# Moving 24 fp32 transposes from the tensor engine to the DMA crossbar in a fused attention and mixture-of-experts kernel

## The chip, the cores and the metric

The kernel runs on one core of a Trainium2 chip. The metric is device time of that core in microseconds (us), lower is better. The margin for "faster" or "slower" is 2%.

The names in the profile: PE is the tensor engine's matmul, PEld its weight loads, DVE the vector engine, ACT the scalar engine, POOL is GpSimd, SP the engine that issues most of the transfers.

## The reference, cut to what matters

```python
# B=4 batches, H=8 heads, S=768 rows, D=64, 16 clusters per head
q_n, k_n, c_n = q/|q|, k/|k|, centroids/|centroids|
q_assign = argmax(einsum('bhsd,hcd->bhsc', q_n, c_n), -1)     # cluster of each query
k_assign = argmax(einsum('bhsd,hcd->bhsc', k_n, c_n), -1)     # cluster of each key
mask   = q_assign[:, :, :, None] == k_assign[:, :, None, :]
attn   = softmax(where(mask, q @ k.T / sqrt(D), -1e9))
x      = (attn @ v) as 3072 x 512
p      = domain_probs / domain_probs.sum(-1)
out    = sum over 4 experts e of p[:, e] * (relu(x @ w1[e]) @ w2[e])   # w1: 512 x 1024
```

Two things matter for the change. Keys and queries have to stand with D on the partitions, so they must be transposed. The cluster scores feed an argmax, so the kernel computes them in fp32: the transposed data must keep all its 32 bits. The two remaining uses of it, the rows for q·k, are cast to bf16.

## The kernel before

One stream of PE instructions interleaves attention, the experts' matmuls and the assignment of the next batch. The batches are numbered 0 to 3; batch 1 is the second. For each batch there are four objects: keys (z = 0) and queries (z = 1) of heads 0 to 3 (g = 0) and of heads 4 to 7 (g = 1). Two classes do the transposing. `Assign.turn` does it on PE, through PSUM (the banks that PE's results go to, from which DVE copies them here); `Crossed` does it with the DMA crossbar in 16-bit elements (the prediction says why), so POOL first splits each fp32 word in its low and high halves, both are crossed, and POOL interleaves them again. The kernel before uses `Crossed` for batches 2 and 3, and `turn` for batches 0 and 1. Each batch's assignment is a list of slots, and the slots are spread over the steps of the attention. The work on each object ends with its onehot, which marks the cluster of each row: one small crossing turns it, and POOL then issues 8 small transfers (the sends) that put it into the rows below the keys or queries. The code is cut down; `...` marks what is left out.

```python
def load_w(e):                       # one expert's weights, issued by POOL
    nc.gpsimd.dma_start(out=W1[e], ...)
    nc.gpsimd.dma_start(out=W2[e], ...)

class Assign:
    def turn(self, y, copy, ...):    # head y of the group: 3 transposes, 1 copy
        tp = self.bank()             # PSUM
        for i in range(3):
            nc.tensor.matmul(tp[:, 128*i:...], raw[b, t, g][:, y, 128*i:...],
                             ident, is_transpose=True)
        t32 = self.all[:, y*384:(y+1)*384]
        copy(t32, tp)                # DVE
    def cast(self, y, r, copy): ...  # bf16 rows for q.k, half r of the partitions (POOL)
    def scores(self, copy): ...      # 4 fp32 matmuls against the centroids, copy
    def back(self): ...              # 3 fp32 transposes of the scores
    def top(self): ...               # onehot of the best cluster (DVE)
    # cross_onehot: DMA transpose of it;  send_all: 8 small transfers, issued by POOL

class Crossed(Assign):
    def split(self, n): ...          # POOL: 128x768 uint16, one half-word plane of 2 heads
    def cross(self, j): ...          # SP: DMA transpose of 128x768 uint16
    def merge(self, n): ...          # POOL: 128x768 uint16 back into self.all
    def casts(self): ...             # DVE: bf16 rows, all four heads at once
    def scores_split(self, bank): ...# scores whose way back also goes by crossbar

def assigns(b):
    xs = [Crossed(b, t, g, ...) for t, g in ((1, 0), (0, 0), (1, 1), (0, 1))]
    def put(at, *fs): ...            # run fs in slot `at` of this batch's list
    for y, x in enumerate(xs):
        z = y % 2
        if b == 1:
            t = 12 * (y // 2) + 4 * z
            for j in range(HG):                      # HG = 4 heads
                put(t + j, lambda x=x, j=j: turn(x, j))
            put(t + 3, lambda: load_raw(upto=13))
            at = 12 * (y // 2) + 8
            put(at, lambda x=x: x.scores(dve))
            put(at + 1 + z, x.back, x.top, x.scale_onehot, x.cross_onehot)
            put(at + 4 + z, x.send_all)
        else: ...                    # split, cross, merge, casts, scores_split
    # weights of experts 2 and 3 in slots 1 and 19, V casts in slots 26 and 29

# the slots of batch 1 (31 of them) are spread evenly over the attention steps
XSTEPS = [0, 31, 63, 63]
gens.append(Paced(assigns(b), XSTEPS[b], S1 + 7, PER_B * b + 2))   # b == 1
```

The softmax here doesn't subtract the row's maximum and nothing guards it: scores larger than these inputs give would overflow.

Of the kernel before, what the change touches and what calls it, by code (L numbers as in the profile page):

```python
# [20 lines left out]
def kernel(  # L21
# [16 lines left out]
    B, H, S, D = q.shape  # L38
# [6 lines left out]
    QW = QT * 128  # L45
# [3 lines left out]
    HG = H // 2  # L49
# [24 lines left out]
    act, dve, pool = nc.scalar.copy, nc.vector.tensor_copy, nc.gpsimd.tensor_copy  # L74
# [35 lines left out]
    def late(t, b):  # L110
        x = KF[b % 2].rearrange("p h r c -> p (h r c)")
        n = NP * A * 128
        return x[:, t * n:(t + 1) * n].rearrange("p (x i r c) -> p x i r c", i=QT, r=2, c=128)
# [15 lines left out]
    def load_part(b, t, g, js=slice(0, HG), c=slice(0, A * D)):  # L129
        nc.sync.dma_start(  # L130
            out=raw[b, t, g][:, js, c],
            in_=(q, k, v)[t][b, g * HG:(g + 1) * HG]
            .rearrange("h (p a) d -> p h (a d)", p=128)[:, js, c])

    def take_raw():
        nonlocal loaded
        x = ORDER[loaded]
        loaded += 1
        raw[x] = raws.tile([128, HG, A * D], F32, name="raw")
        return x  # L140

    def load_raw(n=1, upto=len(ORDER)):
        for _ in range(n):
            if loaded < upto:
                load_part(*take_raw())

    def cast_v(b, g, js=range(HG)):
        for j in js:
            pool(VX[b % 2][:, g * HG + j, :, :D],
                 raw[b, 2, g][:, j, :].rearrange("p (a d) -> p a d", d=D))  # L150

    def load_w(e):
        nc.gpsimd.dma_start(out=W1[e], in_=moe_w1[e].rearrange("(i p) f -> p i f", p=128))
        nc.gpsimd.dma_start(out=W2[e], in_=moe_w2[e].rearrange("(i p) f -> p i f", p=128))
# [57 lines left out]
    class Assign:  # L212
# [23 lines left out]
        def turn(self, y, copy, shared=False):  # L236
            tp = self.bank()
            m, w = self.m, self.w
            for x in range(m):
                for i in range(self.i0, self.i1):  # L240
                    c0 = x * w + (i - self.i0) * 128
                    nc.tensor.matmul(tp[:, c0:c0 + 128],  # L242
                                     raw[self.b, self.t, self.g][:, y * m + x,
                                                                 i * 128:(i + 1) * 128],
                                     ident, is_transpose=True)
            if shared:
                t32 = moe.tile([128, DM], F32, name="t32q", tag="oacc", bufs=4)
            else:
                if self.all is None:
                    self.all = asg.tile([128, HG * QW], F32, name="t32", bufs=2)  # L250
                t32 = self.all[:, y * w:(y + 1) * w]
            copy(t32, tp[:, :m * w])
            self.t32s.append(t32)
# [63 lines left out]
        def put(self, j, r, on):  # L317

            p0 = 2 * CL * j
            self.move(self.rows(slice(D, D + CL), j, r),  # L320
                      self.ot[p0:p0 + CL, r * self.w:(r + 1) * self.w], on)
# [22 lines left out]
    class Crossed(Assign):  # L344


        def halves(self, x):
            return x.rearrange("p j c -> p (j c)").bitcast(U16)

        def split(self, n):  # L350
            src = self.halves(raw[self.b, self.t, self.g]).rearrange(
                "p (y j a d s) -> p s y a j d", j=2, a=A, d=D, s=2)
            if n == 0:
                self.h16 = self.halves(raws.tile([128, HG, QW], F32, name="h16", tag="raw"))
            dst = self.h16.rearrange("p (s y a j d) -> p s y a j d", s=2, a=A, j=2, d=D)
            z, y = divmod(n, HG // 2)
            if self.b == ROWS:
                pool(dst[:, z, y], src[:, z, y])  # L358
            else:
                c = y * 2 * QW  # L360
                pool(self.h16[:, z * HG * QW + c:z * HG * QW + c + 2 * QW],  # L361
                     self.halves(raw[self.b, self.t, self.g])[:, 2 * c:2 * c + 4 * QW][:, z::2])
# [20 lines left out]
        def casts(self):  # L383
            y = self.g * HG // 2
            if self.b < ROWS:
                for r in range(2):
                    dve(self.rows(slice(0, D), slice(0, HG), r),
                        self.all[D * r:D * r + D, :].rearrange("p (j c) -> p j c", j=HG))
                return
            dve(late(self.t, self.b)[:, y:y + HG // 2], self.rows_of())  # L390

        def scores_split(self, bank_tag):
            sc = bank(bank_tag)
            for x in range(HG):
                y, r = divmod(x, 2)
                if self.b == ROWS:
                    lhs, rhs = bdl[:, self.g * HG // 2 + y, :], self.rows_of()[:, y, :, r, :]
                else:
                    lhs, rhs = bdc[:, self.g * HG + x, :], self.all[:, x * QW:(x + 1) * QW]
                nc.tensor.matmul(sc[32 * x:32 * x + 32, :QW], lhs, rhs, start=True, stop=True)  # L400
            self.sch = asg.tile([128, QW], F32, name="scs").bitcast(U16)
            src = sc[:, :QW].bitcast(U16)
            for s in range(2):
                dve(self.sch[:, s * QW:(s + 1) * QW], src[:, s::2])
# [53 lines left out]
    def assigns(b):  # L458


        xs = [Crossed(b, t, g, (("misc",), ("mo",))[t == 0])
              for t, g in ((1, 0), (0, 0), (1, 1), (0, 1))]
        todo = {}

        def put(at, *fs):
            todo.setdefault(at, []).extend(fs)

        def turn(x, j):
            x.turn(j, dve)
            for r in range(2):  # L470
                x.cast(j, r, pool)

        for y, x in enumerate(xs):
            z = y % 2
            if b == 1:
                t = 12 * (y // 2) + 4 * z
                for j in range(HG):
                    put(t + j, lambda x=x, j=j: turn(x, j))
                put(t + 3, lambda: load_raw(upto=13))
                at = 12 * (y // 2) + 8  # L480
            else:
                t = 8 * y
                for j in range(HG):
                    put(t + j, lambda x=x, j=j: x.split(j))
                    put(t + 2 + j, lambda x=x, j=j: x.cross(j))
                    put(t + 9 + j, lambda x=x, j=j: x.merge(j))
                put(t + 6, load_raw)
                put(t + 15 + 4 * z, x.casts)
                at = 16 * (y // 2) + 24
            if b == 1:  # L490
                put(at, lambda x=x: x.scores(dve))
                put(at + 1 + z, x.back, x.top, x.scale_onehot, x.cross_onehot)
                put(at + 4 + z, x.send_all)
                continue
            put(at, lambda x=x, t=("mo", "misc")[z]: x.scores_split(t))
            put(at + 2 + 6 * z, x.cross_scores)
            put(at + 5 + 6 * z, x.merge_scores)
            if b < ROWS:
                put(at + 9 + 6 * z, x.top, x.scale_onehot, x.cross_onehot)
                put(at + 13 + 6 * z, x.send_all)  # L500
                continue
            put(at + 9 + 6 * z, x.top, x.number, x.cross_numbers)
            put(at + 12 + 6 * z, x.store_numbers)
            put(at + 14 + 6 * z, x.spread_numbers)
        for g in range(2):
            if b == 1:
                put(1 + 18 * g, lambda g=g: load_w(2 + g))
                put(26 + 3 * g, lambda g=g: cast_v(b, g), lambda: load_raw(upto=13))
            else:
                for j in range(HG):  # L510
                    put(36 + 8 * g + j, lambda g=g, j=j: cast_v(b, g, (j,)))
                put(40 + 8 * g, load_raw)
        for at in range(XSTEPS[b]):
            for f in todo.pop(at, []):
                f()
            yield
        assert not todo
# [248 lines left out]
    NSTEP = B * UB * PER_U + PAUSE  # L766
    PER_B = UB * PER_U
    LEAD = 6
    XSTEPS = [0, 31, 63, 63]
    step = 0  # L770
    gens = []

# [77 lines left out]
    def late_casts():  # L850
        for j in range(HG):
            cast_v(0, 1, (j,))
            if j < 2:
                casts(k1, (2 + j,))
# [35 lines left out]
    S1 = PER_U + PAUSE  # L890
    gens.append(Paced(late_queries(), 5, S1 - 6, S1 + 4))
    for b in range(1, B):
        gens.append(Paced(assigns(b), XSTEPS[b], PER_B * (b - 1) if b > 1 else S1 + 7,
                          PER_B * b - (2 if b > 1 else -2)))

    def woven(works, upto):

# [51 lines left out]
```

## Time and profile before

The time was 475.53 us (median of 3 runs, 475.3 to 476.02). The page of the profiled execution gives, in short:

| | before |
|---|---|
| span of the profiled execution | 474.3 us |
| busy share: PE / ACT / DVE / POOL | 98% / 58% / 48% / 39% |
| chain that ended last, share of PE | 94% |
| fp32 transposes of raw inputs on PE | 96, of them 48 for batch 1 (3 per head and operand) |
| POOL, from 53.85 to 63.28 us | idle, waiting for the crossed onehot |

How to read it: "busy" is the sum of an engine's instruction records over the span, and an engine can be busy without being the limit. The chain that ended last starts at the last instruction and goes back, at each step, to whatever let that instruction start. When nearly all of that chain is one engine following itself, the time of that engine's stream is the time of the kernel. The lines that show this are in the prediction.

### The profile page before, as it was taken

Reading aid. Unit: us, or ns where it says so; the run is one execution under the profiler, and the core shown is the slowest. Engines: PE = TensorE matmul, PEld = TensorE weight load, DVE = VectorE, ACT = ScalarE, POOL = GpSimd, SP = SyncE. Lnnn points to the kernel's source line nnn. Section 1 sums busy time; section 2 is a strip of 40 time slices with the busy share of each in tenths; the row PEclk is TensorE's granted clock in tenths of the full one; section 3 lists DMA queues with packets and bytes.
Section 4 is the critical chain, followed back from the end, with each engine's and each line's share of the span. In section 5 each row is a group of like instructions: output and inputs, shape, how many; then the busy total and the mean of one; then the engine's idle time right before and its main releaser. Section 6 shows DMA issues by size and latency. Waiting matters only on the chain.

```text
span 474.3 us, 11380 instructions
## 1 busy us (share of the span) xinstructions
PE 466.8 (98%) x4529; PEld 331.6 (70%) x4529; DVE 226.0 (48%) x558; ACT 277.1 (58%) x502; POOL 186.1 (39%) x301
## 2 busy tenths in 40 slices
PE   8999999999999999999999999999999999999997
PEld 4778777776776767677676767776766766667665
DVE  5964764321316664321234544423878767675112
ACT  5757655445665656566565655665665675664442
POOL 5936469180653694450442933000332132220000
PEclk9999999999999999999999999999999999999999
DMA  8999962927664940603657545202100100100101
GB/s 278 259 211 344 241 128 42 177 44 174 96 122 114 199 118 18 159 15 62 150 141 123 115 114 160 68 16 73 50 13 8 54 10 8 36 28 12 44 2 44
DMA packets 75981, 48.27 MB, mean 102 GB/s; under 512 B 51544, under 2 KB 70680, under 8 KB 75928
## 3 DMA queue, kind: packets, MB, share of 16 engines
q1 hardware_dynamic: 66680, 38.22, 32.7%
q0 software_dynamic: 8576, 9.25, 11.0%
q8 instruction: 35, 0.57, 0.6%
q10 hardware_dynamic: 672, 0.08, 0.1%
q14 instruction: 18, 0.15, 0.1%
HBM read 37.31 MB, written 6.30 MB: 92 GB/s over the span
## 4 chain that ended last, share of the span: by engine, by line
PE 94%; DVE 2%; DMA 2%; SPq 0%; issue 0%; ACT 0%; ACTq 0%
PE ps_mo L724 35%; PE ps_mo L743 35%; PE ps_s L634 9%; PE ps_av L661 7%; PE ps_s L547 1%; DMA raw<-in_q_dram 1%; DMA kf<-oht 1%; PE ps_misc L242 1%; PE ps_misc L547 1%; PE ps_misc L400 1%; PE ps_mo L400 1%; PE ps_mo L242 1%; DVE kf L315 1%; PE ps_mo L267 0%; PE ps_misc L267 0%; DVE oh L287 0%
## 5 line engine op out<-in xcount | busy, mean ns | idle before, releaser
L640 ACT ACTIVATE at<-ps_s 128x512 bf16<-128x512 f32 x252 | 147.7, 596 | 119.0 <-PE ps_s L634 103.9
L724 PE MATMUL ps_mo<-xT,w1b 128*128 128x256 bf16 (+1 forms) x1664 | 195.8, 264 | 0.0
L743 PE MATMUL ps_mo<-w2b,hT 128*128 128x512 bf16 (+2 forms) x784 | 190.3, 375 | 0.0
L724 PEld LDWEIGHTS <-w1b 128*128 128x128 bf16 x1664 | 146.3, 98 | 25.1 <-issue 1.2
L730 ACT ACTIVATE hT<-ps_mo 128x512 bf16<-128x512 f32 x192 | 114.7, 598 | 60.7 <-PE ps_mo L724 58.0
L752 DVE SCALAR_TENSOR_TENSOR oacc<-ps_mo,psb,oacc 128x512 f32<-128x512 f32 (+1 forms) x74 | 54.3, 734 | 130.7 <-PE ps_mo L743 130.4
L743 PEld LDWEIGHTS <-hT 128*128 128x128 bf16 x784 | 67.1, 98 | 57.5 <-issue 3.1
L634 PE MATMUL ps_s<-qf,kf 80*128 80x256 bf16 (+1 forms) x456 | 82.5, 267 | 0.9 <-ACT at L640 0.4
L661 PEld LDWEIGHTS <-at 128*128 128x128 bf16 x1152 | 69.9, 97 | 15.3 <-issue 1.7
L661 PE MATMUL ps_av<-vx,at 128*128 128x65 bf16 x1152 | 80.3, 193 | 0.0
L647 POOL TENSOR_TENSOR at<-at,same 128x512 bf16<-128x512 bf16 x24 | 28.2, 1174 | 98.5 <-ACT at L640 82.8
L634 PEld LDWEIGHTS <-kf 80*128 80x128 bf16 x456 | 42.0, 98 | 20.8 <-issue 1.9
L564 DVE TENSOR_SCALAR same<-qf,late 128x256 bf16<-128x256 bf16 x144 | 39.3, 324 | 0.0
L377 POOL COPY t<-t 128x768 uint16<-128x768 uint16 x32 | 35.5, 1116 | 0.0
L647 DVE TENSOR_TENSOR at<-at,same 128x512 bf16<-128x512 bf16 x48 | 21.6, 449 | 25.7 <-ACT at L640 25.7
L358 POOL COPY h<-raw 128x768 uint16<-128x768 uint16 x16 | 13.0, 825 | 37.3 <-DMA raw<-in_q_dram 30.7
L668 DVE RECIPROCAL zr<-ps_av 128x4 f32<-128x4 f32 (+1 forms) x50 | 8.9, 178 | 33.9 <-PE ps_av L661 33.8
L361 POOL COPY h<-raw 128x768 uint16<-128x768 uint16 x16 | 13.0, 826 | 28.9 <-DMA raw<-in_q_dram 20.4
L336 POOL DMA_DIRECT2D kf<-oht x32 | 15.4, 496 | 22.8 <-DMA oht<-oh 13.1
L750 DVE TENSOR_SCALAR oacc<-ps_mo,psb 128x512 f32<-128x512 f32 x18 | 13.5, 749 | 22.7 <-PE ps_mo L743 22.7
L416 POOL COPY st<-sct 128x384 uint16<-128x384 uint16 x16 | 10.6, 708 | 31.7 <-DMA sct<-scs 31.7
L336 POOL DMA_DIRECT2D qf<-oht x40 | 20.0, 509 | 6.2 <-DVE oht L313 3.9
(130 smaller groups left out, 281.5 us busy)
## 6 DMA issues: line engine op xcount, KB each, us to landing
raw<-in_v_dram SPq DMA_DIRECT2D x8, 768.0 KB, 5.7
out_dram<-oacc SPq DMA_DIRECT2D x23, 256.0 KB, 2.2
raw<-in_k_dram SPq DMA_DIRECT2D x7, 768.0 KB, 6.3
raw<-in_q_dram SPq DMA_DIRECT2D x6, 768.0 KB, 5.3
w1b<-in_moe_w_dram POOLq DMA_DIRECT2D x4, 1024.0 KB, 11.5
w2b<-in_moe_w_dram POOLq DMA_DIRECT2D x4, 1024.0 KB, 16.8
qf<-nos SPq DMA_DIRECT2D x2, 768.0 KB, 4.0
xT<-xn SPq DMA_TRANSPOSE x80, 2.4
```

Of the source, the lines that this page charges most:

```text
L336: (nc.gpsimd if self.b or self.i0 and self.g else nc.sync).dma_start(out=self.rows(slice(D, D + CL), j, r), in_=self.oht[p0:p0 + CL, :self.w])
L377: pool(self.all[:, y * w:(y + 1) * w].bitcast(U16)[:, z::2], self.t16[:, (2 * z + y) * w:(2 * z + y + 1) * w])
L564: nc.vector.tensor_scalar(same[:, x * 256:(x + 1) * 256], clusters(b)[:, g, w, k // 2, k % 2, :], key_nos[b % 2][:, g, 8 * i + 4 * (k // 2 ...
L634: nc.tensor.matmul(sp[:, x * n:(x + 1) * n], KF[b % 2][:K, h, r, i * 128:(i + 1) * 128], QF[b % 2][:K, h, rs[0]:rs[-1] + 1, w * 128:(w + 1 ...
L640: nc.scalar.activation(at, sp, ACT.Exp, scale=scale)
L647: (nc.gpsimd if n4 in POOL_STEPS else nc.vector).tensor_tensor(at, at, same_cluster(b, w, cur), op=ALU.mult)
L661: nc.tensor.matmul(av[:, h % 2, m, :], at[:, c0:c0 + 128], VX[b % 2][:, h, 2 * i + r, :], start=(first and x == 0 and m == 0), stop=(last ...
L724: nc.tensor.matmul(ph[:, x * n:(x + 1) * n], W1[e][:, i, (f + x) * 128:(f + x + 1) * 128], xT[:, i, :], start=(i == 0), stop=(i == ND - 1))
L730: nc.scalar.activation(ht, ph, ACT.Relu)
L743: nc.tensor.matmul(po, hT[f // per][:, c0:c0 + 128], W2[e][:, f, c], start=(f == 0), stop=(f == NF - 1))
L750: nc.vector.tensor_scalar_mul(oacc, po, pap)
L752: nc.vector.scalar_tensor_tensor(oacc[:, c], po, pap, oacc[:, c], op0=ALU.mult, op1=ALU.add)
```

## The change

The intent: take the 24 transposes of heads 4 to 7 of batch 1 out of PE's stream and let the crossbar, which has room, do them. Heads 0 to 3 stay on PE. The price is paid on POOL (splits and merges), on SP (eight more crossings) and in the buffers for raw inputs, which now also hold the halves; so the loads of V for heads 4 to 7 and of batch 2's first keys are issued later, and the cluster scores move from slot 20 to slot 29 of a list that has 38 slots now.

```diff
--- before.py
+++ after.py
@@ -347,6 +347,9 @@
         def halves(self, x):
             return x.rearrange("p j c -> p (j c)").bitcast(U16)
 
+        def take_all(self):
+            self.t32s = [self.all[:, j * QW:(j + 1) * QW] for j in range(HG)]
+
         def split(self, n):
             src = self.halves(raw[self.b, self.t, self.g]).rearrange(
                 "p (y j a d s) -> p s y a j d", j=2, a=A, d=D, s=2)
@@ -384,10 +387,13 @@
             y = self.g * HG // 2
             if self.b < ROWS:
                 for r in range(2):
-                    dve(self.rows(slice(0, D), slice(0, HG), r),
-                        self.all[D * r:D * r + D, :].rearrange("p (j c) -> p j c", j=HG))
+                    self.cast_half(r)
                 return
             dve(late(self.t, self.b)[:, y:y + HG // 2], self.rows_of())
+
+        def cast_half(self, r):
+            dve(self.rows(slice(0, D), slice(0, HG), r),
+                self.all[D * r:D * r + D, :].rearrange("p (j c) -> p j c", j=HG))
 
         def scores_split(self, bank_tag):
             sc = bank(bank_tag)
@@ -470,28 +476,41 @@
             for r in range(2):
                 x.cast(j, r, pool)
 
-        for y, x in enumerate(xs):
-            z = y % 2
-            if b == 1:
-                t = 12 * (y // 2) + 4 * z
-                for j in range(HG):
-                    put(t + j, lambda x=x, j=j: turn(x, j))
-                put(t + 3, lambda: load_raw(upto=13))
-                at = 12 * (y // 2) + 8
-            else:
-                t = 8 * y
-                for j in range(HG):
-                    put(t + j, lambda x=x, j=j: x.split(j))
-                    put(t + 2 + j, lambda x=x, j=j: x.cross(j))
-                    put(t + 9 + j, lambda x=x, j=j: x.merge(j))
-                put(t + 6, load_raw)
-                put(t + 15 + 4 * z, x.casts)
-                at = 16 * (y // 2) + 24
-            if b == 1:
+        if b == 1:
+            for y, x in enumerate(xs):
+                g, z = divmod(y, 2)
+                if g == 0:
+                    for j in range(HG):
+                        put(4 * z + j, lambda x=x, j=j: turn(x, j))
+                else:
+                    for j in range(HG):
+                        put((8, 14)[z] + j, lambda x=x, j=j: x.split(j))
+                        put((13, 18)[z] + j, lambda x=x, j=j: x.cross(j))
+                        put((20, 24)[z] + j, lambda x=x, j=j: x.merge(j))
+                    put((24, 28)[z], x.take_all)
+                    for r in range(2):
+                        put(28 + 3 * z + r, lambda x=x, r=r: x.cast_half(r))
+                at = (8, 29)[g]
                 put(at, lambda x=x: x.scores(dve))
                 put(at + 1 + z, x.back, x.top, x.scale_onehot, x.cross_onehot)
-                put(at + 4 + z, x.send_all)
-                continue
+                put(at + (4, 5)[g] + z, x.send_all)
+            put(1, lambda: load_w(2))
+            put(3, lambda: load_raw(upto=11))
+            put(20, lambda: cast_v(b, 0))
+            put(22, lambda: load_raw(2, upto=13))
+            put(24, lambda: load_w(3))
+            put(30, lambda: cast_v(b, 1))
+
+        for y, x in enumerate(xs if b > 1 else ()):
+            z = y % 2
+            t = 8 * y
+            for j in range(HG):
+                put(t + j, lambda x=x, j=j: x.split(j))
+                put(t + 2 + j, lambda x=x, j=j: x.cross(j))
+                put(t + 9 + j, lambda x=x, j=j: x.merge(j))
+            put(t + 6, load_raw)
+            put(t + 15 + 4 * z, x.casts)
+            at = 16 * (y // 2) + 24
             put(at, lambda x=x, t=("mo", "misc")[z]: x.scores_split(t))
             put(at + 2 + 6 * z, x.cross_scores)
             put(at + 5 + 6 * z, x.merge_scores)
@@ -502,14 +521,10 @@
             put(at + 9 + 6 * z, x.top, x.number, x.cross_numbers)
             put(at + 12 + 6 * z, x.store_numbers)
             put(at + 14 + 6 * z, x.spread_numbers)
-        for g in range(2):
-            if b == 1:
-                put(1 + 18 * g, lambda g=g: load_w(2 + g))
-                put(26 + 3 * g, lambda g=g: cast_v(b, g), lambda: load_raw(upto=13))
-            else:
-                for j in range(HG):
-                    put(36 + 8 * g + j, lambda g=g, j=j: cast_v(b, g, (j,)))
-                put(40 + 8 * g, load_raw)
+        for g in range(2 if b > 1 else 0):
+            for j in range(HG):
+                put(36 + 8 * g + j, lambda g=g, j=j: cast_v(b, g, (j,)))
+            put(40 + 8 * g, load_raw)
         for at in range(XSTEPS[b]):
             for f in todo.pop(at, []):
                 f()
@@ -766,7 +781,7 @@
     NSTEP = B * UB * PER_U + PAUSE
     PER_B = UB * PER_U
     LEAD = 6
-    XSTEPS = [0, 31, 63, 63]
+    XSTEPS = [0, 38, 63, 63]
     step = 0
     gens = []
 
@@ -891,7 +906,7 @@
     gens.append(Paced(late_queries(), 5, S1 - 6, S1 + 4))
     for b in range(1, B):
         gens.append(Paced(assigns(b), XSTEPS[b], PER_B * (b - 1) if b > 1 else S1 + 7,
-                          PER_B * b - (2 if b > 1 else -2)))
+                          PER_B * b - 2 if b > 1 else S1 + 55))
 
     def woven(works, upto):
 
```

## The prediction

> **What bounds the kernel now.** I read the page's engine table and its slices first, then the chain that ended last, then the groups of instructions with shapes kept apart, then the timeline of the stretch that the change touches. The engine table and the head of the slices:
>
> ```profile
> PE 466.8 (98%) x4529; PEld 331.6 (70%) x4529; DVE 226.0 (48%) x558; ACT 277.1 (58%) x502; POOL 186.1 (39%) x301
> ...
> PE   8999999999999999999999999999999999999997
> ...
> POOL 5936469180653694450442933000332132220000
> PEclk9999999999999999999999999999999999999999
> DMA  8999962927664940603657545202100100100101
> ```
>
> PE is busy in every slice after the first at full granted clock; no other engine is over 58%. Busy alone does not prove a bound, so the chain that ended last is what carries it:
>
> ```profile
> PE 94%; DVE 2%; DMA 2%; SPq 0%; issue 0%; ACT 0%; ACTq 0%
> ```
>
> 94% of the span is PE following PE in program order, so an instruction taken out of PE's stream in the middle of the kernel shortens the span by the time it holds that stream, as long as what replaces it is there when PE asks. In the waits of PE between 30 and 130 us there is one entry only, 0.2 us for a onehot tile. So PE has almost no waiting to give up: the gain is pure removed work, and any new wait is a pure loss.
>
> **What the Trainium skill says.** "TensorE: Matmul & The Clock Gate", Part 4, says that PE's transpose goes to PSUM, so that a copy must follow, and gives about 275 ns for a 128x128 one inside a kernel. The trace agrees on the record (273 ns for fp32) but the records overlap: three hold the stream for only 0.36 us. "DMA: Bandwidth & Descriptors", DMA Transpose (X-bar), Constraints: only 2-byte elements and only from SP or ACT. That is why the fp32 data is split in halves; in this trace the same trick in batches 2 and 3 is uint16 and issued by SP. "Trainium Kernel Development and Optimization", Key Constraints: transfers issued from SP, ACT and POOL share the same 16 DMA engines. The trace agrees: while expert 2's weights and raw loads were in flight together (45 to 57 us), the second weight half took 15.9 us to land against 13.7 us for expert 3's, alone.
>
> **The change, part by part.** It concerns keys and queries of heads 4 to 7 of batch 1. Each of the two has 4 heads x 3 blocks of 128x128, so 24 fp32 transposes leave PE. Their place is in the PE timeline, in sets of three:
>
> ```profile
> 58.46 0.52 PE L242 MATMUL ps_misc<-ident,raw 128*128 128x128 f32 x3
> 58.82 0.59 PE L743 MATMUL ps_mo<-w2b,hT 128*128 128x512 bf16 x2
> ...
> 66.71 0.53 PE L242 MATMUL ps_mo<-ident,raw 128*128 128x128 f32 x3
> 67.08 1.47 PE L724 MATMUL ps_mo<-xT,w1b 128*128 128x256 bf16 x12
> ```
>
> The cost is start to next start, not the record's 0.52: the eight sets give 0.36, 0.39, 0.33, 0.38, 0.36, 0.37, 0.38 and 0.37, in sum **2.94 us**. This lies wholly on PE's path. The fp32 cluster scores and the two transposes back stay on PE and move later: scores from position 68.82 to behind the start of expert 2's second unit.
>
> DVE loses 8 copies of 128x384 from PSUM at 0.555 us (4.4 us) and gains 4 casts of 64x1536 at 1.1 us (4.4 us): even. POOL loses 16 casts of 64x384 at 0.505 us (8.1 us) and gains 8 splits at 0.826 (6.6 us) and 8 merges at 1.04 to 1.12 (8.6 us): **7 us more**. SP's queue gains 8 crossbar transposes at 1.25 us of issue and 2.8 us to landing. Loads of V (heads 4 to 7) and of batch 2's first keys move later, because their buffers now hold the halves. Expert 3's weights are issued further on in the program. None of these is on PE's path as long as it is in time.
>
> **Is it in time?** The rows that decide it are the groups of the pieces and POOL's timeline:
>
> ```profile
> L377 POOL COPY t<-t 128x768 uint16<-128x768 uint16 x32 | 35.5, 1116 | 0.0
> L361 POOL COPY h<-raw 128x768 uint16<-128x768 uint16 x16 | 13.0, 826 | 28.9 <-DMA raw<-in_q_dram 20.4 <-DMA raw<-in_k_dram 8.4
> ...
> 63.28 3.86 POOL L336 DMA_DIRECT2D kf<-oht  x8 [9.43 <-DMA oht<-oh]
> 67.19 1.05 POOL L258 CAST kf<-t 64x384 bf16<-64x384 f32 x2
> 68.18 3.81 POOL L336 DMA_DIRECT2D qf<-oht  x8
> 72.04 3.23 POOL L258 CAST kf<-t 64x384 bf16<-64x384 f32 x6
> 75.31 4.32 POOL L258 CAST qf<-t 64x384 bf16<-64x384 f32 x8
> 79.57 0.81 POOL L153 DMA_DIRECT2D w1b<-in_moe_w_dram  x1
> ```
>
> POOL works in order and sits from 53.85 to 63.28 us waiting for the crossed onehot of heads 0 to 3. The order of the changed kernel puts the key splits into that hole (53.9 to 57.2, free), then the 16 sends, the query splits, one merge, 4 V casts, three merges, one merge of queries, expert 3's two weight issues, three merges.
>
> My clock for that. In the kernel before, the onehot transposes (issued 56.9) queue behind the V load issued at 46.63 (11.3 us) and share the engines with expert 2's weights; the change moves that V load away, so I estimate that the onehot lands at 60.5 rather than 63.3. Sends 16 x 0.49 = 7.8: to 68.3. Query splits 3.3: to 71.6. Merge 1.05 and V casts 2.0: 74.7. Three merges: 78. First query merge 79, weights 1.7: 80.8, three merges: **84.0**. The transposes of the query halves can only start at 71.6; with two xT transposes between them (2.4 us) the last is issued near 78 and lands near 81, just ahead of its merge.
>
> PE comes to those scores at: 89.93 in the timeline before (88.28, the pieces of that step, then 8 of the 24 matmuls), less 2.94, less the group's own scores (1.43) and transposes back (0.66) that no longer stand ahead of them: **84.9**. So the data is there 0.9 us ahead by my estimate, and late by 1.9 us if the onehot does not land sooner than before. That is the tightest point. Weighing these, I take a mean wait of 0.4 us.
>
> The second point is expert 3. Its issue at 79 to 80 is where it was (79.57), but V and K loads of 1.5 MB now run beside it. Alone it took 13.7 us for the second half; expert 2's, with such loads beside it, 15.9. So about 96 to 97 against PE's need at 103.47 - 2.94 = 100.5: no wait.
>
> Sum: 475.5 - 2.9 + 0.4 = **473.0 us**, 0.5% faster.
>
> **The rivals.**
> First: **PE waits at the moved scores** because POOL's 7 us more come in a stretch where POOL is already solid (63 to 84). For it: a margin below 1 us, and an in-order queue with a DMA wait at its head. Against it: the hole before 63 takes the key splits, and 16 casts go. It gives back 1 to 3 us: 474 to 476.
> Second: **expert 3's weights late**, through DMA contention or a late POOL. For it: the weights are issued behind a merge that itself waits for a transpose. Against: 3.5 us of margin. It would cost 1 to 3 us more.
> Third: **nothing takes its place**: the whole 2.94 is kept, 472.6. The slots look chosen to just fit, which speaks for it. A fourth, that removal leaves PE waiting for ACT between closer steps, I hold small: ACT is at 58% and it waits for PE 104 us at the exps.
>
> **Range and chances.** The best case is 472.6, and 0.3 us of noise in the runs makes 472.0 the low end. The bad case of the first rival, 475, is the high end; beyond it both rivals have to hit. Over 2% means under 466, four times the removed work: chance 0.01. Over 2% slower means 485, some 12 us of new stalls, which needs a wait that repeats or a load that comes far too late: 0.02.
>
> **What the profile after would show.** Right: the fp32 transposes of the stretch 58 to 67 gone (96 to 72 by count at that line); PE's time before heads 4 to 7 shorter by 2.9; PE's waits still under a microsecond; POOL's sends of the onehot starting near 60.5; merges done by 84. Wrong: a wait of PE at the scores matmul for POOL's merge (first rival), or at the first matmuls of expert 3 for its weights (second), or a span that shrinks by less than 2.9 with no wait of PE, which would say that the sets did not cost 0.36 each. The prediction fails as a whole if PE stalls by more than 2.5 us in sum, or if the time falls below 472.0, for which something besides the transposes would have to leave PE's path.

## The result, and the profile after

| | before | after |
|---|---|---|
| time, median (range) | 475.77 us (475.3 to 476.12), 4 runs | 472.21 us (472.15 to 472.63), 4 runs |
| ratio after / before, 95% interval | | 0.993 (0.9916 to 0.9944) |
| span of the profiled execution | 474.3 us | 470.4 us |

Ratios here and below are the mean time of one kernel's fast runs over the mean of the other's fast runs of the same rounds, so they are not quite the ratio of the medians quoted. The kernel is 0.7% faster and counts as the same at the 2% margin.

From the page of the changed kernel: the engine table, two rows of the 40 slices, and the engines of the chain that ended last.

```profile
PE 463.2 (98%) x4505; PEld 329.1 (70%) x4505; DVE 227.4 (48%) x554; ACT 276.9 (59%) x502; POOL 194.8 (41%) x301
...
POOL 5936779275355593450433942000233232230000
...
DMA  8999966996645941503666844220100100100101
...
PE 95%; DVE 2%; DMA 1%; issue 0%; ACT 0%; SPq 0%; ACTq 0%
```

PE has 24 matmuls fewer (4529 to 4505; the raw transposes at L242 go from 96 to 72) and 3.6 us less busy time, and is still 94 to 95% of the chain. POOL has 8.7 us more; I had counted 7. In its row the fifth to seventh digits rise from 469 to 779: the former hole, around 54 to 63 us, holds the key splits now. In the row of the DMA engines the seventh digit rises from 2 to 6, where most of the added crossings and the moved loads begin, and the ninth from 2 to 9: there expert 3's weights are still under way (they landed at 97.96 and before at 94.07), and batch 2's crossings begin at 97.4 and not at 103.2.

The timeline of PE in the changed kernel (start, duration, engine, line, operation, tiles, count), first where a set of three transposes stood, then where heads 4 to 7's scores stand:

```profile
58.18 0.29 PE L676 MATMUL ps_av<-vx,at 128*128 128x65 bf16 x4
58.31 0.59 PE L758 MATMUL ps_mo<-w2b,hT 128*128 128x512 bf16 x2
58.74 0.38 PE L649 MATMUL ps_s<-qf,kf 80*128 80x256 bf16 x2
...
84.14 0.61 PE L739 MATMUL ps_mo<-xT,w1b 128*128 128x128 bf16 x8
84.68 0.85 PE L267 MATMUL ps_misc<-t,bdc 128*32 128x384 f32 x8
85.35 0.83 PE L267 MATMUL ps_mo<-t,bdc 128*32 128x384 f32 x8
```

Before, a set of matmuls of the attention weights with V (`ps_av`) started at 58.34 and the next set of an expert's second matmuls (`w2b`) at 58.82, with the transposes at 58.46 between them; now one follows the other after 0.13 us. The scores of the keys start at 84.68, those of the queries at 85.35, and neither line carries a wait in brackets.

POOL's timeline in the changed kernel, which has to feed those scores; the bracket is the idle time before a group and what ended it:

```profile
53.75 3.13 POOL L364 COPY h<-raw 128x768 uint16<-128x768 uint16 x4
...
60.96 3.87 POOL L336 DMA_DIRECT2D kf<-oht  x8 [4.08 <-DMA oht<-oh]
65.13 3.83 POOL L336 DMA_DIRECT2D qf<-oht  x8 [0.30 <-DMA kf<-oht]
68.96 3.12 POOL L364 COPY h<-raw 128x768 uint16<-128x768 uint16 x4
...
80.33 3.73 POOL L380 COPY t<-t 128x768 uint16<-128x768 uint16 x3
```

The key splits sit where POOL was idle, the onehot came at 60.96 instead of 63.28, and the last merge ended at 80.33 + 3.73 = 84.06, which is 1.3 us before the query scores that need it.

**Where the time went.** Single spans differ by chance at the start and near the end of the program, so I measured one stretch that holds the whole change and none of that. Its first mark is POOL's pair of key casts of heads 0 to 3 near 44 us, its second the first fp32 scores of batch 3. The two marks before, and then after:

```profile
44.57 1.05 POOL L258 CAST kf<-t 64x384 bf16<-64x384 f32 x2 [0.76 <-DVE t L252]
254.10 0.85 PE L400 MATMUL ps_mo<-t,late 128*32 128x384 f32 x8
...
44.41 1.05 POOL L258 CAST kf<-t 64x384 bf16<-64x384 f32 x2 [0.77 <-DVE t L252]
250.95 0.85 PE L406 MATMUL ps_mo<-t,late 128*32 128x384 f32 x8
```

In the profile before it ran from 44.57 to 254.10, which is 209.53 us; in the one after from 44.41 to 250.95, which is 206.54. So **2.99 us of the 3.9 us between the two spans lie in the stretch**; 0.16 lie ahead of it, and 0.75 behind it (220.2 us from the second mark to the end, against 219.45). The experiments treat the 2.99 and the 0.75 separately.

### The profile page after: what moved, and what is told of

It reads as the page before. It is cut to its first block, busy times and chain, and to the rows that moved or that the text cites. A ratio compares the mean times of both kernels' runs of the same rounds, so it can differ in the third digit from the quotient of the medians.

```text
span 470.4 us, 11349 instructions
## 1 busy us (share of the span) xinstructions
PE 463.2 (98%) x4505; PEld 329.1 (70%) x4505; DVE 227.4 (48%) x554; ACT 276.9 (59%) x502; POOL 194.8 (41%) x301
## 4 chain that ended last, share of the span: by engine, by line
PE 95%; DVE 2%; DMA 1%; issue 0%; ACT 0%; SPq 0%; ACTq 0%
PE ps_mo L739 36%; PE ps_mo L758 35%; PE ps_s L649 9%; PE ps_av L676 7%; PE ps_s L562 1%; DMA kf<-oht 1%; PE ps_misc L562 1%; PE ps_s L87 1%; PE ps_mo L406 1%; PE ps_mo L242 1%; PE ps_misc L406 1%; DVE kf L315 1%; PE ps_misc L242 1%; PE ps_mo L267 0%; PE ps_misc L267 0%; DVE oh L287 0%
## 5 line engine op out<-in xcount | busy, mean ns | idle before, releaser
L745 ACT ACTIVATE hT<-ps_mo 128x512 bf16<-128x512 f32 x192 | 114.7, 598 | 60.5 <-PE ps_mo L739 57.7
L380 POOL COPY t<-t 128x768 uint16<-128x768 uint16 x40 | 44.3, 1127 | 0.0
L364 POOL COPY h<-raw 128x768 uint16<-128x768 uint16 x24 | 20.3, 864 | 30.4 <-DMA raw<-in_k_dram 16.7
L361 POOL COPY h<-raw 128x768 uint16<-128x768 uint16 x16 | 13.1, 829 | 39.3 <-DMA raw<-in_q_dram 32.3
L685 DVE TENSOR_TENSOR xn<-ps_av,zr 128x256 bf16<-128x256 f32 (+1 forms) x50 | 20.7, 414 | 1.7
```

Source lines behind the costliest of these rows:

```text
L380: pool(self.all[:, y * w:(y + 1) * w].bitcast(U16)[:, z::2], self.t16[:, (2 * z + y) * w:(2 * z + y + 1) * w])
L685: nc.vector.tensor_tensor(xn[:, :nr].rearrange("p i j d -> p j i d"), av[:, :, :, :D], zr.broadcast_to([128, 2, nr, D]), op=ALU.mult)
L745: nc.scalar.activation(ht, ph, ACT.Relu)
```

## The experiments

The theory: the gain is the time that the 24 transposes held PE's stream and nothing else, and POOL and the DMA stay ahead with a small margin. Its rivals: (a) some of the gain comes from the moved loads and the new slots, not from the removed transposes; (b) PE gains more and gives part of it back in a new wait. Later a third question came up: what the 0.75 us outside the stretch is. Every run gave a correct result.

The measure in each case is the ratio to the kernel before of the same rounds, and the stretch defined above, whose noise is shown by the controls.

### Controls: ctl_before and after_again

No edit: the kernel before, and the changed kernel, run again.

> The kernel before, unchanged, as a control. Every theory expects a ratio of 1.000 within 0.002. What it is to tell: in the profile of the kernel before, PE lost 0.7 us at the last fp32 cluster scores of batch 3 (282.90 to 284.38 us, 1.48 us for 8 matmuls where the first 8 took 0.66), because the crossed scores before landed 5.5 us after their issue; in the changed kernel they landed in 3.7 us and the wait was gone. If this wait is a property of the schedule, it shows here again; if it is chance of one execution, it is absent or of another size.

> The changed kernel, unchanged, in the same rounds as its improved version. The transposes theory, with 3.0 us saved between 44 and 254 us and nothing lasting elsewhere, expects ratio 0.9935 to 0.994; the first measurement, 0.993 over few runs, should come down toward it. If there is a lasting second gain of half a microsecond: 0.9925 to 0.993.

Measured: ctl_before 475.49 us against 475.56 (ratio 0.9996, 0.9983 to 1.001), stretch 209.54. after_again 472.17 against 475.53 (0.9928, 0.9916 to 0.994; six runs against ten), stretch 206.54. The stretch repeats within 0.01 us in both kernels (two profiles of each), so it is a far finer measure than the time of a run. The difference of the two is 3.00 us. The ratio of after_again did not come down toward 0.994 as I expected; it lies in the band that I had given to a second gain of half a microsecond. Its profile shows no such gain after the stretch, though: from the second mark to the end it took 219.5 us, as in ctl_before.

### sched_only: the new slots and loads, with the transposes still on PE

```diff
-                        put((8, 14)[z] + j, lambda x=x, j=j: x.split(j))
-                        put((13, 18)[z] + j, lambda x=x, j=j: x.cross(j))
-                        put((20, 24)[z] + j, lambda x=x, j=j: x.merge(j))
-                    put((24, 28)[z], x.take_all)
-                    for r in range(2):
-                        put(28 + 3 * z + r, lambda x=x, r=r: x.cast_half(r))
+                        put((12, 16)[z] + j, lambda x=x, j=j: turn(x, j))
```

> The schedule of the change alone (38 slots, later scores, V and K loads and weights in their new places), with heads 4 to 7 still turned by PE and cast by POOL. Transposes theory: ratio to before 0.998 to 1.000 (at most the 0.7 us wait of batch 3 goes). Rival that the schedule itself brings it: 0.993 to 0.995.

Measured: 475.36 us, ratio 0.9995 (0.9982 to 1.0007), stretch 209.54. The schedule alone is worth nothing. Rival (a) falls.

### keys_only: only the keys of heads 4 to 7 go by the crossbar

```diff
-                if g == 0:
+                if g == 0 or z == 1:
                     for j in range(HG):
-                        put(4 * z + j, lambda x=x, j=j: turn(x, j))
+                        put(12 * g + 4 * z + j, lambda x=x, j=j: turn(x, j))
```

> Only the keys of heads 4 to 7 go through the crossbar; the queries are turned by PE, in the schedule of the change. Transposes theory, linear in the sets: half of 2.94, so 1.5 us (with batch 3's wait gone 2.2): ratio 0.9955 to 0.997. Rival, all or nothing by the schedule: 0.993.

Measured: 473.43 us, ratio 0.9955 (0.9943 to 0.9968), stretch 207.99, which is 1.54 us less than before. Half of the transposes bring half of the gain: the gain is proportional to what is removed, as removed work is and as a wait need not be.

### idle_turns: the change, and 24 transposes of the identity put back on PE

The three transposes per head read and write nothing that anything waits for; they only hold the stream.

```diff
+        def idle_turn(x):
+            tp = x.bank()
+            for i in range(QT):
+                nc.tensor.matmul(tp[:, i * 128:(i + 1) * 128], ident, ident, is_transpose=True)
...
+                    for j in range(HG):
+                        put((12, 16)[z] + j, lambda x=x: idle_turn(x))
```

> The changed kernel plus the 24 fp32 transposes put back at about their old places as idle work on PE (identity into a bank that nobody reads). Theory that the gain is PE time of 24 transposes: 2.9 to 3.0 us more than the changed kernel, so about 475.2 us, ratio to before 0.999. Rival that the gain comes from the other movements (V load later, POOL and DMA order, batch 3's wait gone): stays at 472 to 473, ratio 0.993 to 0.994.

Measured: 475.05 us, ratio 0.9988 (0.9975 to 1.0001), stretch 209.30: 2.76 us of the 2.99 come back. The crossbar path is all in place here, so it is PE's stream that was relieved. The 24 idle ones cost 0.115 us each and the real ones 0.125. Of the 0.23 us between the sums, about 0.1 lies in the sets themselves: from start to next start the idle ones sum to 2.83 us. The rest was not looked for.

### scores_28: the scores of heads 4 to 7 one slot earlier

```diff
-                at = (8, 29)[g]
+                at = (8, 28)[g]
```

This tests whether the margin at the scores is small, that is whether the slot is chosen to just fit.

> The changed kernel with the moved scores, and the steps after them that hang on the same slot, one slot (about 1.26 steps) earlier. In the changed kernel the last merge ends at 84.06 and PE is at the first scores at 84.68. PE would now come to them some 2 us sooner, near 82.5. Theory of a margin of about half a microsecond: PE waits 1 to 2 us for the last merge of the queries, ratio to before 0.995 to 0.997 (473.3 to 474.2 us). Rival that PE has ample slack here: ratio stays 0.993.

Measured: 474.8 us, ratio 0.9984 (0.9972 to 0.9997), stretch 209.19, which is 2.65 us worse than the change. PE's timeline:

```profile
81.28 0.85 PE L267 MATMUL ps_misc<-t,bdc 128*32 128x384 f32 x8
81.95 0.82 PE L267 MATMUL ps_mo<-t,bdc 128*32 128x384 f32 x4
...
84.59 0.84 PE L267 MATMUL ps_mo<-t,bdc 128*32 128x384 f32 x4 [1.82 <-POOL t L380]
```

The keys' eight matmuls and half of the queries' run without a wait, and the other four start 2.64 us after those, when POOL's last merges are done. In the change they follow at once, so this wait is the whole loss. This is the first rival of my prediction, made real: one slot earlier, nearly the whole gain is gone. PE came 3.4 us earlier than in the change (81.28 against 84.68), where I had reckoned with 2, because the step between the two slots is a long block, and POOL's last merge ended at 84.53, 0.47 later than in the change; so the cost was more than I expected.

### v_early: an idle 768 KB load about where the V load was, ahead of the crossed onehot

```diff
+            put(4, lambda: nc.sync.dma_start(
+                out=W1[3].rearrange("p i f -> p (i f)").bitcast(F32)[:, :HG * A * D]
+                .rearrange("p (j c) -> p j c", j=HG),
+                in_=v[1, HG:].rearrange("h (p a) d -> p h (a d)", p=128)))
```

The real V load cannot simply go back, as its buffer holds the halves. So this loads the same bytes into the room of expert 3's first weights, which are written later. It was issued earlier than the load that it stands for: it ran from 39.62 to 55.90 us, the V load before from 46.63 to 57.88. It tests the part of the prediction that said the onehot lands sooner because the V load is gone.

> The changed kernel plus an idle load of 768 KB of V in front of the crossed onehot of heads 0 to 3 (into the room of expert 3's weights, which come later), so that the traffic there is as in the kernel before. Theory of the prediction: the onehot lands near 63.3 instead of 61.0, the merges end near 86.4, PE waits about 1.7 us at the scores: ratio to before 0.996 to 0.9975. Rival that expert 2's weights alone set the landing: 61.0 again and 0.993.

Measured: 472.79 us, ratio 0.9944 (0.9932 to 0.9957), stretch 207.63, which is 1.09 us worse than the change. POOL's timeline:

```profile
63.29 3.86 POOL L336 DMA_DIRECT2D kf<-oht  x8 [6.31 <-DMA oht<-oh]
...
82.66 2.98 POOL L380 COPY t<-t 128x768 uint16<-128x768 uint16 x3
```

And PE's timeline, at the first of expert 3's second matmuls:

```profile
101.52 1.02 PE L762 MATMUL ps_mo<-w2b,hT 128*128 128x512 bf16 x3 [0.72 <-ACT hT L749]
```

The onehot came at 63.29, within 0.01 us of where it came before the change. That the moved V load brings it forward by 2.3 us is right. The way was not quite the predicted one, a queue behind V: here the idle load had landed at 55.90, before the crossings of the onehot were issued at 57.13 and 58.74. What was late was expert 2's second weight transfer: it landed at 62.30 (62.29 before, 59.73 in the change). In all twelve profiles that transfer landed at 62.3 to 62.7 us where the V or idle load ran ahead, and at 59.7 to 60.1 where it did not, and POOL's first send of the onehot followed 0.9 to 1.3 us later. The size of the loss was not as I expected. The merges ended at 85.64 instead of 84.06, only 1.6 us later, because POOL made up some time, and PE lost 0.24 us at the query scores, not 1.7. It stood idle for 0.72 us elsewhere, at the first matmul of expert 3's second weights. The profile puts that wait down to ACT, but the transfer of those weights was issued at 81.42 and took 20.0 us to land, to 101.4. So the second rival of the prediction showed here: in the change itself that transfer was issued at 79.44, took 18.5 us and landed at 97.96, with PE needing it at 100.3, and here it was issued 2.0 us later, as POOL was late, and took 1.5 us longer. Priced from start to next start, this wait cost 0.86 us (2.22 from the start of the 24 matmuls ahead of it, against 1.36 in the change), and with the 0.24 that is the whole of the 1.09.

### scores_cross and scores_cross2: the scores' way back by crossbar too

An attempt to find a better version: the three fp32 transposes back per object (`back`) also leave PE, as in batches 2 and 3.

```diff
+                if g == 1:
+                    put(29, lambda x=x, t=("misc", "mo")[z]: x.scores_split(t))
+                    put(30 + 2 * z, x.cross_scores)
+                    put(31 + 2 * z, x.merge_scores)
+                    put(33 + 2 * z, x.top, x.scale_onehot, x.cross_onehot)
+                    put(36 + 2 * z, x.send_all)
+                    continue
...
-    XSTEPS = [0, 38, 63, 63]
+    XSTEPS = [0, 39, 63, 63]
```

> The changed kernel, and the scores of heads 4 to 7 go back through the crossbar as halves too, in place of two sets of three fp32 transposes on PE (0.33 us each). If it is in time: 0.66 us less than the changed kernel, ratio to before 0.991 to 0.992. Rival: the onehot of these heads comes too late (it passes POOL behind expert 3's weights and batch 2's keys), PE waits at heads 4 to 7, and the time is equal or up to 3 us more.

Measured: 473.46 us, ratio 0.996 (0.9946 to 0.9973), stretch 207.65: 1.11 us worse than the change, though 0.66 us of work left PE. POOL's timeline:

```profile
99.82 1.14 POOL L422 COPY st<-sct 128x384 uint16<-128x384 uint16 x2 [6.18 <-DMA sct<-scs]
```

And PE's timeline at batch 2's first query scores:

```profile
140.06 0.82 PE L406 MATMUL ps_misc<-t,bdc 128*32 128x384 f32 x4
141.81 0.84 PE L406 MATMUL ps_misc<-t,bdc 128*32 128x384 f32 x4 [0.94 <-POOL t L380]
```

POOL works in order. The first crossing of scores, issued at 87.29 while expert 3's weights were under way (they landed at 99.59), took 12.5 us to land. POOL stood still for 6.18 us in front of it, so batch 2's splits and merges behind it came late, and 40 us later the second four score matmuls start 1.75 us after the first four, where they would follow at once. That wait is, within 0.02, the sum of the 0.66 us removed and the 1.11 lost. So I moved batch 2's first scores by two slots:

```diff
-            at = 16 * (y // 2) + 24
+            at = 16 * (y // 2) + 24 + (2 if b == 2 and y < 2 else 0)
```

> The variant whose scores of heads 4 to 7 also go back through the crossbar, with the first scores of batch 2 two slots later. In the variant without that PE waited 1.8 us at those scores of batch 2 for POOL's merges (from 140.7 to 141.8 us and before its weight loads), because POOL had waited for the crossed scores. If that wait is the whole loss: 0.66 us less than the changed kernel, ratio to before 0.992 to 0.9927. If POOL's lateness travels on to batch 2's next scores or heads: 0.9935 or worse.

Measured: 473.85 us, ratio 0.9956 (0.9942 to 0.9969), stretch 208.12. The wait at the scores is gone and another took its place. DVE's timeline:

```profile
128.89 1.92 DVE L395 CAST kf<-t 64x1536 bf16<-64x1536 f32 x2 [4.64 <-POOL t L380]
```

And from the list of waits (who waited, for whom: us in total, times, longest):

```profile
PE ps_mo L745 <- DVE oacc L771: 1.9, 2, 1.3
```

Now DVE, which also works in order, stands 4.64 us in front of a cast for the same late merges; its next work, adding the experts' outputs, comes late, and PE waits 1.9 us for a PSUM bank. Removing 0.66 us from PE has cost 1.1 to 1.6. The version of the change stays the best that I found.

### b3_later: the 0.75 us outside the stretch

Edit, against the kernel before: batch 3's last scores one slot later.

```diff
-            put(at, lambda x=x, t=("mo", "misc")[z]: x.scores_split(t))
+            put(at + (b == ROWS and y > 1), lambda x=x, t=("mo", "misc")[z]: x.scores_split(t))
```

The reason lies in two profiles of one and the same kernel. In the first profile of the kernel before, PE's timeline near 283 us is:

```profile
282.90 1.55 PE L400 MATMUL ps_misc<-t,late 128*32 128x384 f32 x8
284.38 1.04 PE L743 MATMUL ps_mo<-w2b,hT 128*128 128x512 bf16 x4
```

and POOL's, which feeds it:

```profile
280.19 1.14 POOL L416 COPY st<-sct 128x384 uint16<-128x384 uint16 x2 [8.38 <-DMA sct<-scs]
281.24 2.31 POOL L377 COPY t<-t 128x768 uint16<-128x768 uint16 x2
```

PE's timeline in the profile of ctl_before, the same program:

```profile
283.20 0.83 PE L400 MATMUL ps_misc<-t,late 128*32 128x384 f32 x8
283.96 1.04 PE L743 MATMUL ps_mo<-w2b,hT 128*128 128x512 bf16 x4
```

and POOL's:

```profile
278.19 1.14 POOL L416 COPY st<-sct 128x384 uint16<-128x384 uint16 x2 [6.10 <-DMA sct<-scs]
279.25 2.31 POOL L377 COPY t<-t 128x768 uint16<-128x768 uint16 x2
```

In the first, the crossed query scores of heads 0 to 3, which POOL handles ahead of the merges, came at 280.19, its merges ended at 283.55, and the eight score matmuls held PE from 282.90 to 284.38, which is 1.48 us. In the second they came two us sooner, the merges ended at 281.56, and the same eight held it for 0.76 us. So an execution of the kernel before loses **0.7 us by chance**. Over the twelve profiles, this one crossing landed after 3.3 to 3.7 us (nine profiles, those of ctl_before and of the change among them) or after 5.1 to 5.3 us (three: this one, idle_turns and b3_later), with nothing between. In the change, PE comes to those scores at 279.76 with the merges done by 278.0, in a profile where the crossing was quick. What its schedule would lose with a slow one, idle_turns shows, which has the same batch 3: the merges ended at 282.64, and the eight score matmuls held PE for 1.03 us from 282.43, which is 0.27 lost and not 0.72.

> The kernel before with the fp32 scores of heads 4 to 7 of batch 3 one slot later. If PE's wait of 0.7 us there is in every execution of the kernel before: 0.5 to 0.7 us less, ratio 0.9985 to 0.999. If it is chance of one execution: 1.000 within 0.0005.

Measured: 475.2 us against 475.46, ratio 0.9996 (0.9984 to 1.0009), stretch 209.54. Its crossing was one of the slow ones (5.1 us), and PE still did not wait there; the part behind the stretch took 219.46 us, as in ctl_before (219.5). So the slot removes the wait in the profile. In the times it does not stand out from the noise, and the run is inconclusive as to what the wait costs on average.

## Why the prediction was right, point by point

- **PE's own stream is the bound: shown.** Removing half or all of the transposes takes 1.54 and 3.0 us off the stretch, putting idle ones back returns 2.76, and moving everything but the transposes (sched_only) does nothing.
- **2.94 us from the eight intervals, start to next start: right within 0.06.** The stretch shrank by 2.99 and 3.00. Adding the records themselves would have given 24 x 0.273 = 6.6 us, over twice too much.
- **POOL 7 us more, DVE even: nearly.** POOL had 8.7 us more and DVE 1.4. The added splits came to 7.3 us and not 6.6, the merges to 8.8 as against 8.6. As POOL's hole took the key splits, this cost nothing.
- **The clock of POOL: right.** Sends from 60.96 (60.5 estimated), merges done at 84.06 (84.0), PE at the scores at 84.68 (84.9). That the end fits to 0.06 is partly luck: the sends started 0.46 us late, the next four merges took 3.8 us where I took 4.3, and the last three 3.7 where I took 3.2. v_early shows that the moved V load is what brings the onehot forward, but by way of expert 2's weights, which land sooner without it, and not by a queue behind V.
- **First rival, a wait at the scores: it did not happen, and here a term of the sum was off.** I put 0.4 us for it as a mean of cases; it was 0. I also took the margin from the key scores, where it would be 0.6 us. The last merges belong to the queries, whose matmuls start 0.67 us later, and so it was 1.3. That the margin is thin was right: scores_28 turns it into a loss of 2.65 us.
- **Second rival, expert 3's weights: it did not happen, and it was closer than I said.** The second half took 18.5 us to land and not 15.9. It was there at 97.96 (96 to 97 estimated) and PE needed it at 100.3, so the margin was 2.3 us and not 3.5. v_early used it up.
- **Third rival, the whole 2.94 is kept: this is what came.** It gave 472.6; the runs gave 472.2, against my 473.0 and inside 472.0 to 475.0.
- **The rest is 0.4 to 0.6 us that I did not have.** The medians of the two pairs of timings differ by 3.56 and 3.36 us, the stretch by 3.0. The chance wait of 0.7 us in batch 3, which some executions of the kernel before pay, is a cause that the traces show in single executions; with a slow crossing the schedule of the change lost 0.27 us (idle_turns). I counted it for no kernel. The fastest run of the kernel before in all rounds was 475.09 and of the change 472.15: 2.94 apart. That fits, but how often each kernel pays that wait was not measured, and the start of the program also shifts by up to 0.8 us between profiles (the first mark lay between 44.30 and 45.07). The split of the last half microsecond stays open.

## What to carry to other kernels

When one engine's stream is the bound, price an instruction by the time from its start to the next one's start in the timeline, not by its record: that gave a gain of 3 us to within 2%. Then work out a clock for the engine that must feed the replacement, including the waits at the head of its in-order queue, and compare it with the moment when the data is asked for; here the margin was 1.3 us, one slot earlier lost nearly all of the gain, and moving 0.66 us more off PE cost over a microsecond elsewhere. For a gain well under one per cent, measure between two marks inside the trace: here the stretch repeated to 0.01 us in two profiles of each kernel, where whole runs varied by 1.

## What the Trainium skill lacked or had wrong

- "TensorE: Matmul & The Clock Gate", Part 4, gives about 275 ns for a PE transpose in a kernel's context. The record of an fp32 one here is as long (273 ns, the median; the page's figure stands beside one for bf16), but the page has no figure for how long a transpose holds the stream: inside a set of three the next one started after 0.109 us, and 24 of them were worth 2.99 us, 0.125 us each, less than half of the record.
- "DMA: Bandwidth & Descriptors", DMA Transpose (X-bar), lists constraints and no times; a time for one block stands elsewhere ("VectorE: DVE Perf Modes", The three transpose paths: 1309 ns for 128x128 bf16). No page that I read says how much longer a crossing takes beside loads. In the change one of 128x768 16-bit elements took 1.24 us of SP's queue (median of 40) and 2.8 us from issue to landing, up to 5.8 us, and the one of 128x384 that was issued beside expert 3's weights (scores_cross) took 12.5 us.
- No page that I read speaks of a crossing that lands after one of two times in the same program: the crossing of batch 3's query scores of heads 0 to 3 took 3.3 to 3.7 us in nine profiles and 5.1 to 5.3 us in three others, with no edit needed to change from one to the other. The next crossing, 10 to 13 us later, took anything from 2.9 to 5.5 us in the same twelve, so the two times are a finding about that one crossing. Its cause is open.
